# A fused attention and gated-MLP block: the first unit's queries in two pairs of heads, and the first modulation weight split along the contraction

## The chip, the cores and the metric

The kernel runs on one core of a Trainium2 chip. The core has five engines that run side by side and meet at semaphores: TensorE (matrix products, into PSUM banks), VectorE, ScalarE, GpSimd and SyncE, which here only issues DMAs. ScalarE and GpSimd issue DMAs too. Every engine takes its instructions in program order. The metric is the device time of one execution in microseconds.

## The reference

A transformer block with conditioned normalisation: attention with grouped heads (2048 queries, 32 query heads of 128 on 8 key/value heads, 2048 keys), then a gated MLP that mixes along the sequence. All inputs are bfloat16.

```
mod = (_silu(c) @ w_mod).reshape(c.shape[0], 6, 1, -1)
sa, ca, ga, sb, cb, gb = (mod[:, i] for i in range(6))
h = _layernorm(x, axis=-1) * (1 + ca) + sa
x = x + ga * _A_ref(h, A_k_cache, A_v_cache, A_wq, A_wo)
h = _layernorm(x, axis=-1) * (1 + cb) + sb
x = x + gb * _B_ref(h, B_w_in, B_w_sp, B_b_sp, B_w_out)

# _A_ref
q = (x @ wq), split into 32 heads
scores = q k^T * Dh ** -0.5
p = softmax(scores)
return (p v), heads joined, @ wo
```

What the change touches is the very start: `sa` and `1 + ca` (the first 1024 columns of `w_mod`), the normalised first rows of x, their queries for the first four heads, and the first scores.

## The kernel before

Attention runs in 128 **units**: 8 key/value heads times 16 tiles of 128 queries, each unit with its four query heads. The main loop (L1375) goes over iterations `it`; each has 8 slots. In slot i of iteration it, `qk(it, i)` makes the scores of unit `it` and ScalarE's exp of them, `pv_part` the values of the unit before, and further work is put in by hand: `later[(it, i)]` (by `at`) runs ahead of the scores of that slot, `fill[(it, i)]` behind its values. The order of each engine is the order of the program (`manual_schedule`, L634).

`qk` for unit 0 (L1024 to L1038): per slot two matmuls with the keys of one tile of 128 as weights and the queries of all four heads as 512 columns, into one of two PSUM pieces `s_ps`, and one exp of 128x1024 into `pTs[0]`. So slot i covers key tiles 2i and 2i + 1, for all four heads.

**What comes ahead of the loop.** SyncE's queue loads, in order: the first modulation weight `wmod_a` in two halves by output columns (L707; columns of `sa`, then those of `ca`), the query weight of the first group `wqs[0]` in two halves by contraction tiles (L752), the first half of the natural keys `k_nat` (L712), x tile 1 (L754), the second half of `k_nat`, x tiles 2 and 3 (L756), the other keys by a transposing DMA (L760), values and the rest of x. ScalarE's queue loads c and x tile 0 (L703, L704).

Then, on the engines:

- `warm(n)` (L784): n matmuls with zeros into a bank of `o_ps` that nobody reads. They keep TensorE at work.
- VectorE and GpSimd make the statistics of x tile 0 (`ln_stats`, L698 and L699), its 1/std (`rstd_of`, L679 and L683) and VectorE the normalised rows xn (L687).
- `mod_part` (L857): for each of the 4 output tiles of one modulation vector, 4 matmuls over the contraction, each with one column. It runs once for `sa`, once for `ca`. `mod_copy` (L867, L868) copies the one, and copies the other with 1 added.
- Four transposes of xn (L894), two scale-and-shift steps on VectorE (L816) and two on ScalarE (L908) give `hT`, the first tile of h, turned.
- Queries of all four heads (L921, 16 matmuls, in the middle of which `k_turn` turns key tiles 0 to 3, L879 and L882); VectorE copies two heads' queries and ScalarE two (L929).
- `first = dict(r1=ln1_stats(1, 1))` (L962): statistics of x tile 1.

**In iteration 0**, `first_norm` (L1198, behind the scores of slot 0) turns key tiles 4 to 7 and has the statistics of x tiles 2 and 3 and the normalised rows of tile 1; `first_turn` (ahead of slot 3) transposes tile 1 (`ln1_turn`, L834, with the scale-and-shift L816) and normalises tiles 2 and 3; `ln1_turn(2, 2)` stands ahead of slot 6. Slots 4 and 5 have the queries of tile 1 (`next_q`, L947, copied in L958), slot 7 the first of those of tiles 2 and 3 (`rest_q`). Slots 1 to 3 have one warm matmul each.

The few lines that matter most:

```
first = dict(r1=ln1_stats(1, 1))
...
def first_norm():
    k_turn((4, 5, 6, 7), (nc.vector.tensor_copy,))
    ln_stats(mv1, 2, x_sb[:, 2, :])
    first["x1"] = ln1_norm(1, 1, first["r1"])
    ln_stats(mv1, 3, x_sb[:, 3, :])
    first["r2"] = rstd_of(mv1[:, 2:4, :], 2, "ln1")
...
at(0, 3, first_turn)
at(0, 6, lambda: ln1_turn(2, 2, first["x2"]))
fill[0, 0] = [first_norm]
```

Of the kernel before, what the change touches and what calls it, by code (L numbers as in the profile page):

```python
# [12 lines left out]
ACT = mybir.ActivationFunctionType  # L13
# [562 lines left out]
def kernel(  # L576
# [93 lines left out]
    def bank(name):  # L670
        return psum.tile([P, 512], FP32, name=name)
# [30 lines left out]
    c_bf = res.tile([P, NDT], BF16, name="c_bf")  # L702
    nc.scalar.dma_start(out=c_bf[:], in_=c_dram)  # L703
    nc.scalar.dma_start(out=x_sb[:, 0, :], in_=x_dram[:, 0, :])  # L704
    for i in range(2):
        part = slice(i * D, (i + 1) * D)
        nc.sync.dma_start(out=wmod_a[:, :, part], in_=wmod_dram[:, :, part])  # L707
    k_nat = early.tile([P, SK], BF16, name="kT")

    def load_k_nat(half):  # L710
        t0, t1 = half * NKT // 4, (half + 1) * NKT // 4
        nc.sync.dma_start(  # L712
            out=k_nat[:, t0 * P : t1 * P].rearrange("p (t d) -> p t d", d=DH),
            in_=k_rows[:, t0:t1, :],
        )
# [32 lines left out]
    nc.gpsimd.memset(mhalf[:], -0.5)  # L748
    make_identity(nc, ident[:])
    wqs[0] = early.tile([P, NDT, REP * DH], BF16, name="wq_g")  # L750
    for dts in (slice(0, 2), slice(2, 4)):
        nc.sync.dma_start(out=wqs[0][:, dts, :], in_=wq_dram[:, dts, 0 : REP * DH])  # L752
    load_k_nat(0)
    nc.sync.dma_start(out=x_sb[:, 1, :], in_=x_dram[:, 1, :])  # L754
    load_k_nat(1)
    nc.sync.dma_start(out=x_sb[:, 2:CT, :], in_=x_dram[:, 2:CT, :])  # L756
# [125 lines left out]
            copy(out=kT0[:, part[0] * P : (part[-1] + 1) * P], in_=k_ps[:, 0 : n * P])  # L882


    xns0 = ln1_norm(0, 1, ln1_stats(0, 1))
    mc_ps = bank("misc")
    warm(10)
    mod_part(0, wmod_a, 0, mc_ps)
    warm(6)
    mod_part(1, wmod_a, D, mc_ps)  # L890

    x_ps = [bank("misc")[:].bitcast(BF16), bank2()[:, 0:512].bitcast(BF16)]
    for dt in range(NDT):
# [2 lines left out]
            xns0[0][:, dt * P : (dt + 1) * P],  # L896
            ident[:],
        )
    mod_copy(0, mc_ps)
    warm(2)  # L900
    hT_of(0)
    for k in range(2):
# [10 lines left out]
                    bias=modc[:, dt : dt + 1],  # L913
                )
    qTs = {0: early.tile([P, REP, 512], BF16, name="qT")}
    q_ps = [bank("misc"), bank2()]
    for dt in range(NDT):
        if dt == 2:
            k_turn((0, 1, 2, 3), (nc.vector.tensor_copy, nc.scalar.copy))
        for hh in range(REP):  # L920
            nc.tensor.matmul(  # L921
                q_ps[hh // 2][:, hh % 2 * P : (hh % 2 + 1) * P],
                lhsT=wqs[0][:, dt, hh * DH : (hh + 1) * DH],
                rhs=hTs[0][:, dt, 0:P],
                start=(dt == 0 and hh % 2 == 0),
                stop=(dt == NDT - 1 and hh % 2 == 1),
            )
    for hf, copy in enumerate((nc.vector.tensor_copy, nc.scalar.copy)):
        copy(  # L929
            out=qTs[0][:, 2 * hf : 2 * hf + 2, 0:P],  # L930
            in_=q_ps[hf][:, 0 : 2 * P].rearrange("p (h q) -> p h q", h=2),
        )
    warm(2)

    def qproj(b, heads, c0, n, banks=("misc", "misc")):

# [22 lines left out]

        return [lambda hh=hh, dt=dt: mm(hh, dt) for hh in heads for dt in range(NDT)]  # L960

    first = dict(r1=ln1_stats(1, 1))  # L962


    NU = HKV * NT
# [26 lines left out]
    def qk(u, i):  # L992
        g, j = divmod(u, NT)
        b, jj = g * NCH + j // CT, j % CT
        if i == 0:
            if homes[u] == "wsp":
                pTs[u] = wspp.tile([P, NT, 512], BF16, name="wsp")
            else:
                pTs[u] = late.tile([P, NKT, 512], BF16, name=homes[u], bufs=1)
            if by_rows(u):  # L1000
                rsums[u] = stat.tile([P, NSLOT], FP32, name="rs")
        s_ps = bank2()
        if by_rows(u):
            hh, half = divmod(i, 2)
            for c in range(2):
                k0 = (2 * half + c) * 512
                nc.tensor.matmul(  # L1007
                    s_ps[:, c * 512 : (c + 1) * 512],
                    lhsT=qTs[b][:, hh, jj * P : (jj + 1) * P],
                    rhs=groups[g]["kT"][:, k0 : k0 + 512],  # L1010
                    start=True,
                    stop=True,
                )
            nc.scalar.activation(  # L1014
                out=rows_of(u, hh)[:, half * HK : (half + 1) * HK],
                in_=s_ps[:],
                func=ACT.Exp,
                scale=inv_sqrt_dh,
                accum_out=rsums[u][:, i : i + 1],
            )  # L1020
            if half == 1:
                at(*divmod(u * NSLOT + i + 2, NSLOT), lambda: turn_rows(u, hh))
            return
        for h in range(2):  # L1024
            kt = 2 * i + h
            nc.tensor.matmul(  # L1026
                s_ps[:, h * 512 : (h + 1) * 512].rearrange("p (r q) -> p r q", r=REP),
                lhsT=groups[g]["kT"][:, kt * P : (kt + 1) * P],
                rhs=qTs[b][:, :, jj * P : (jj + 1) * P],
                start=True,  # L1030
                stop=True,
            )
        nc.scalar.activation(  # L1033
            out=pTs[u][:, 2 * i : 2 * i + 2, :],
            in_=s_ps[:].rearrange("p (k q) -> p k q", k=2),
            func=ACT.Exp,
            scale=inv_sqrt_dh,
        )  # L1038
# [157 lines left out]

    fill = {}
    def first_norm():  # L1198
        k_turn((4, 5, 6, 7), (nc.vector.tensor_copy,))
        ln_stats(mv1, 2, x_sb[:, 2, :])  # L1200
        first["x1"] = ln1_norm(1, 1, first["r1"])
        ln_stats(mv1, 3, x_sb[:, 3, :])
        first["r2"] = rstd_of(mv1[:, 2:4, :], 2, "ln1")
# [386 lines left out]
```

## Time and profile before

| | us |
|---|---|
| median of 3 runs | 1311.61 (1310.94 to 1311.62) |
| the profiled execution | 1311.72 |
| its span, first to last instruction | 1309.7 |
| first modulation weight, first half, used by TensorE from | 5.40 |
| its second half, from | 7.43 |
| first scale-and-shift (L816) | 8.36 |
| first score matmul of unit 0 (L1026) | 10.63 |
| first exp (L1033) | 11.26 |
| first score matmul of unit 1 | 18.36 |

All times within the profile count from the start of the span. A row of a timeline gives an instruction's start, its length, engine, line, operation, what it writes and reads, and in brackets how long its engine had been idle before it and what ended that. Consecutive like instructions are put together ("x6"): then the length is from the first one's start to the last one's end. On TensorE the ends are modelled: the next matmul starts before the shown end of the one before, so the step from start to start is what a matmul costs in a stream. A chain of waits is followed back from the last instruction of the execution: each piece was released by the one above it. A row of waits gives the total, how many there were, and the longest.

### The profile page before, as it was taken

To read this page: it belongs to the slowest core of one execution; us is meant where nothing else is said; L and a number is where in the kernel's file an instruction comes from. 1 tells how busy PE (TensorE), PEld (TensorE's weight loads), DVE (VectorE), ACT (ScalarE), POOL (GpSimd) and SP (SyncE) were. 2 spreads that over 40 slices of the span, in tenths; PEclk is the share of its full clock that TensorE was granted. 3 is DMA by queue.
4 is the path that set the end of the run, shared out by engine and by line. 5 is a ranking of instruction groups with operands and counts; after the bars stand their busy time and mean duration, and the time that the engine had idled before them with its cause. 6 is when DMAs were issued, how large, how long until landed. Compare 5 with 4: busy or idle time off the path is not lost.

```text
span 1309.7 us, 24370 instructions
## 1 busy us (share of the span) xinstructions
PE 1301.9 (99%) x9527; PEld 736.3 (56%) x9527; DVE 684.2 (52%) x1693; ACT 1112.4 (85%) x1533; POOL 58.7 (4%) x116
## 2 busy tenths in 40 slices
PE   9999999999999999999999999999999999999998
PEld 5665555555555555555555555555555555644445
DVE  6544544444445454444454544444555588784443
ACT  7899999999999999999999999999999999550000
POOL 1200000000000000000000000000000011120000
PEclk9999999999999999999999999999999999999999
DMA  7668778877887677867986678678776688464300
GB/s 181 153 94 154 129 127 159 154 126 133 153 168 143 126 139 155 145 130 137 169 160 127 125 156 156 128 137 153 163 144 124 119 141 147 105 134 96 85 21 31
DMA packets 607723, 174.45 MB, mean 133 GB/s; under 512 B 597264, under 2 KB 603664, under 8 KB 607600
## 3 DMA queue, kind: packets, MB, share of 16 engines
q1 hardware_dynamic: 600576, 153.67, 65.0%
q0 software_dynamic: 4432, 16.91, 4.2%
q10 hardware_dynamic: 2592, 2.23, 0.5%
q8 instruction: 77, 1.26, 0.4%
q14 instruction: 46, 0.38, 0.1%
HBM read 21.89 MB, written 2.10 MB: 18 GB/s over the span
## 4 chain that ended last, share of the span: by engine, by line
PE 97%; DMA 2%; DVE 1%; POOL 0%; issue 0%; ACT 0%; SPq 0%; DVEq 0%
PE o_ps L1082 18%; PE s_ps L1026 18%; PE s_ps L1007 16%; PE o_ps L1061 16%; PE misc L1114 8%; PE misc L947 8%; PE misc L1457 7%; PE s_ps L1292 2%; PE s_ps L1331 2%; PE o_ps L1490 1%; DMA wsp<-in_w_mod_dram 1%; PE s_ps L1490 0%; DMA wmod_a<-in_w_mod_dram 0%; DMA hT<-xn 0%; DVE hT L816 0%; DVE bnst L698 0%
## 5 line engine op out<-in xcount | busy, mean ns | idle before, releaser
L1033 ACT ACTIVATE pT<-s_ps 128x1024 bf16<-128x1024 f32 x552 | 560.4, 1024 | 32.1 <-PE s_ps L1026 10.1
L1082 PEld LDWEIGHTS <-pT 128*128 128x128 bf16 x4416 | 295.3, 98 | 128.9
L1082 PE MATMUL o_ps<-v,pT 128*128 128x129 bf16 x4416 | 339.7, 220 | 0.0
L1026 PE MATMUL s_ps<-qT,kT 128*128 128x512 bf16 x1104 | 328.1, 379 | 0.3 <-ACT pT L1033 0.2
L1007 PE MATMUL s_ps<-kT,qT 128*128 128x512 bf16 x944 | 280.7, 379 | 0.1
L1014 ACT ACTIVATE win_sb<-s_ps 128x1024 bf16<-128x1024 f32 x238 | 243.4, 1024 | 3.5
L1114 PE MATMUL misc<-wo_g,oT 128*128 128x512 bf16 x512 | 194.0, 379 | 0.0
L947 PE MATMUL misc<-hT,wq_g 128*128 128x512 bf16 (+2 forms) x520 | 187.0, 371 | 0.1
L1026 PEld LDWEIGHTS <-kT 128*128 128x128 bf16 x1104 | 107.2, 98 | 115.0 <-issue 2.3
L1014 ACT ACTIVATE pn<-s_ps 128x1024 bf16<-128x1024 f32 x156 | 159.4, 1023 | 2.0 <-ACT wmod_a L1014 0.3
L1061 PEld LDWEIGHTS <-v 128*128 128x128 bf16 x944 | 92.3, 98 | 111.5
L958 DVE CAST qT<-misc 128x512 bf16<-128x512 f32 x125 | 85.6, 685 | 123.5 <-PE misc L947 123.5
L1070 DVE CAST oT<-o_ps 128x512 bf16<-128x512 f32 x59 | 40.8, 691 | 195.0 <-PE o_ps L1061 195.0
L1061 PE MATMUL o_ps<-wsp,v 128*128 128x512 bf16 x480 | 142.1, 379 | 0.0
L1061 PE MATMUL o_ps<-pT,v 128*128 128x512 bf16 x464 | 138.0, 379 | 0.0
L1007 PEld LDWEIGHTS <-qT 128*128 128x128 bf16 x944 | 92.2, 98 | 61.7 <-issue 0.2
L1047 DVE TENSOR_TENSOR tot<-rs 128x1 f32<-128x1 f32 x236 | 36.1, 153 | 127.3 <-ACT win_sb L1014 84.9
L1457 PE MATMUL misc<-wsp,z 128*128 128x512 bf16 (+2 forms) x560 | 100.5, 336 | 0.0
L1052 DVE TENSOR_SCALAR win_sb<-win_sb,rall 128x2048 bf16<-128x2048 bf16 x119 | 89.6, 753 | 4.4 <-DVE rall L1050 0.3
L1014 ACT ACTIVATE wmod_a<-s_ps 128x1024 bf16<-128x1024 f32 x78 | 79.8, 1023 | 0.0
L1457 PEld LDWEIGHTS <-z 128*128 128x128 bf16 x560 | 50.5, 98 | 48.4 <-issue 0.2
L1127 DVE TENSOR_TENSOR xacc<-misc,xacc 128x512 f32<-128x512 f32 x112 | 76.0, 679 | 0.0
(111 smaller groups left out, 817.4 us busy)
## 6 DMA issues: line engine op xcount, KB each, us to landing
v<-in_A_v_cache_dram POOLq DMA_DIRECT2D x7, 512.0 KB, 6.6
wq_g<-in_A_wq_dram POOLq DMA_DIRECT2D x7, 512.0 KB, 4.9
wo_g<-in_A_wo_dram POOLq DMA_DIRECT2D x7, 512.0 KB, 4.3
wsp<-in_w_mod_dram POOLq DMA_DIRECT2D x1, 2048.0 KB, 11.8
out_dram<-yout ACTq DMA_DIRECT2D x16, 128.0 KB, 1.7
win_sb<-in_B_w_in_dram POOLq DMA_DIRECT2D x1, 1792.0 KB, 8.1
x_sb<-in_A_x_dram SPq DMA_DIRECT2D x3, 512.0 KB, 8.1
oT<-onorm SPq DMA_TRANSPOSE x69, 2.8
```

The source lines that it names most:

```text
L947: nc.tensor.matmul(ps[0][:, o0 : o0 + n], lhsT=wqs[g][:, dt, hh * DH : (hh + 1) * DH], rhs=hTs[ch][:, dt, c0 : c0 + n], start=(dt == 0), s ...
L958: nc.vector.tensor_copy(out=dst, in_=src)
L1007: nc.tensor.matmul(s_ps[:, c * 512 : (c + 1) * 512], lhsT=qTs[b][:, hh, jj * P : (jj + 1) * P], rhs=groups[g]["kT"][:, k0 : k0 + 512], sta ...
L1014: nc.scalar.activation(out=rows_of(u, hh)[:, half * HK : (half + 1) * HK], in_=s_ps[:], func=ACT.Exp, scale=inv_sqrt_dh, accum_out=rsums[u ...
L1026: nc.tensor.matmul(s_ps[:, h * 512 : (h + 1) * 512].rearrange("p (r q) -> p r q", r=REP), lhsT=groups[g]["kT"][:, kt * P : (kt + 1) * P], ...
L1033: nc.scalar.activation(out=pTs[u][:, 2 * i : 2 * i + 2, :], in_=s_ps[:].rearrange("p (k q) -> p k q", k=2), func=ACT.Exp, scale=inv_sqrt_dh,)
L1052: nc.vector.tensor_scalar(out=rows, in0=rows, scalar1=rinv, scalar2=None, op0=ALU.mult)
L1061: nc.tensor.matmul(o_pss[u][:], lhsT=groups[g]["v1"][:, kt, 0:DH], rhs=pTs[u][:, kt, :], start=(kt == 0), stop=(kt == NKT - 1),)
L1082: nc.tensor.matmul(o_ps[:, hh % 2, 0 : DH + 1], lhsT=pTs[u][:, kt, hh * P : (hh + 1) * P], rhs=groups[g]["v1"][:, kt, 0 : DH + 1], start=( ...
L1114: nc.tensor.matmul(X_ps[:], lhsT=oTs[u][:, hh, :], rhs=groups[g]["wo"][:, hh, :], start=(hh == 0), stop=(hh == REP - 1),)
L1127: nc.vector.tensor_tensor(out=xaccs[j][:], in0=X_ps[:], in1=xaccs[j][:], op=ALU.add)
L1457: nc.tensor.matmul(g_pss[f][:, :n], lhsT=z2[:, st, f * P : (f + 1) * P], rhs=wsp[t][:, st, c0 : c0 + n], start=(st == 0), stop=(st == NT - ...
```

## The change

The first modulation weight is loaded as three contraction tiles (all 1024 columns) and then the last one, instead of two halves of the columns. `mod_first(kt)` makes the 8 one-column matmuls of one contraction tile; with the first tile goes a matmul of a matrix of 1/128 with ones, which puts the added 1 into the columns of `ca`. Three tiles run ahead of the transposes of x tile 0, the last behind them, and one copy replaces the two.

The first group's query weight is loaded by pairs of heads, in rows of 256 columns, with the first half of the natural keys between the two. `first_q(hf)` makes and copies the queries of one pair, always on VectorE. The first pair is made ahead of the loop, the second in `first_norm`, behind the scores of slot 0. Unit 0's `qk` goes by pairs: slot i has four key tiles and the pair i % 2, four matmuls of 256 columns. Key tiles 0 and 1 are copied by ScalarE and 2 and 3 by VectorE (the other way round before). The statistics of x tile 1 move from ahead of the loop into `first_norm`, behind the copy of key tiles 4 to 7.

```diff
--- before.py
+++ after.py
@@ -702,9 +702,8 @@
     c_bf = res.tile([P, NDT], BF16, name="c_bf")
     nc.scalar.dma_start(out=c_bf[:], in_=c_dram)
     nc.scalar.dma_start(out=x_sb[:, 0, :], in_=x_dram[:, 0, :])
-    for i in range(2):
-        part = slice(i * D, (i + 1) * D)
-        nc.sync.dma_start(out=wmod_a[:, :, part], in_=wmod_dram[:, :, part])
+    for kts in (slice(0, NDT - 1), slice(NDT - 1, NDT)):
+        nc.sync.dma_start(out=wmod_a[:, kts, :], in_=wmod_dram[:, kts, 0 : 2 * D])
     k_nat = early.tile([P, SK], BF16, name="kT")
 
     def load_k_nat(half):
@@ -748,9 +747,10 @@
     nc.gpsimd.memset(mhalf[:], -0.5)
     make_identity(nc, ident[:])
     wqs[0] = early.tile([P, NDT, REP * DH], BF16, name="wq_g")
-    for dts in (slice(0, 2), slice(2, 4)):
-        nc.sync.dma_start(out=wqs[0][:, dts, :], in_=wq_dram[:, dts, 0 : REP * DH])
+    pairs = [slice(2 * hf * DH, 2 * (hf + 1) * DH) for hf in range(2)]
+    nc.sync.dma_start(out=wqs[0][:, :, pairs[0]], in_=wq_dram[:, :, pairs[0]])
     load_k_nat(0)
+    nc.sync.dma_start(out=wqs[0][:, :, pairs[1]], in_=wq_dram[:, :, pairs[1]])
     nc.sync.dma_start(out=x_sb[:, 1, :], in_=x_dram[:, 1, :])
     load_k_nat(1)
     nc.sync.dma_start(out=x_sb[:, 2:CT, :], in_=x_dram[:, 2:CT, :])
@@ -882,12 +882,30 @@
             copy(out=kT0[:, part[0] * P : (part[-1] + 1) * P], in_=k_ps[:, 0 : n * P])
 
 
+    def mod_first(kt, mc_ps):
+        for col in range(2 * NDT):
+            nc.tensor.matmul(
+                mc_ps[:, col : col + 1],
+                lhsT=wmod_a[:, kt, col * P : (col + 1) * P],
+                rhs=sc_bf[:, kt : kt + 1],
+                start=(kt == 0 and col == 0),
+                stop=(kt == NDT - 1 and col == 2 * NDT - 1),
+            )
+        if kt == 0:
+            nc.tensor.matmul(
+                mc_ps[:, NDT : 2 * NDT],
+                lhsT=mean_bf[:],
+                rhs=ones_bf[:, 0:NDT],
+                start=False,
+                stop=False,
+            )
+
     xns0 = ln1_norm(0, 1, ln1_stats(0, 1))
     mc_ps = bank("misc")
-    warm(10)
-    mod_part(0, wmod_a, 0, mc_ps)
-    warm(6)
-    mod_part(1, wmod_a, D, mc_ps)
+    warm(12)
+    for kt in range(NDT - 1):
+        mod_first(kt, mc_ps)
+    warm(1)
 
     x_ps = [bank("misc")[:].bitcast(BF16), bank2()[:, 0:512].bitcast(BF16)]
     for dt in range(NDT):
@@ -896,7 +914,8 @@
             xns0[0][:, dt * P : (dt + 1) * P],
             ident[:],
         )
-    mod_copy(0, mc_ps)
+    mod_first(NDT - 1, mc_ps)
+    nc.vector.tensor_copy(out=modc[:, 0 : 2 * NDT], in_=mc_ps[:, 0 : 2 * NDT])
     warm(2)
     hT_of(0)
     for k in range(2):
@@ -913,24 +932,26 @@
                     bias=modc[:, dt : dt + 1],
                 )
     qTs = {0: early.tile([P, REP, 512], BF16, name="qT")}
-    q_ps = [bank("misc"), bank2()]
-    for dt in range(NDT):
-        if dt == 2:
-            k_turn((0, 1, 2, 3), (nc.vector.tensor_copy, nc.scalar.copy))
-        for hh in range(REP):
-            nc.tensor.matmul(
-                q_ps[hh // 2][:, hh % 2 * P : (hh % 2 + 1) * P],
-                lhsT=wqs[0][:, dt, hh * DH : (hh + 1) * DH],
-                rhs=hTs[0][:, dt, 0:P],
-                start=(dt == 0 and hh % 2 == 0),
-                stop=(dt == NDT - 1 and hh % 2 == 1),
-            )
-    for hf, copy in enumerate((nc.vector.tensor_copy, nc.scalar.copy)):
-        copy(
+
+    def first_q(hf):
+        q_ps = bank("misc")
+        for dt in range(NDT):
+            for k in range(2):
+                hh = 2 * hf + k
+                nc.tensor.matmul(
+                    q_ps[:, k * P : (k + 1) * P],
+                    lhsT=wqs[0][:, dt, hh * DH : (hh + 1) * DH],
+                    rhs=hTs[0][:, dt, 0:P],
+                    start=(dt == 0 and k == 0),
+                    stop=(dt == NDT - 1 and k == 1),
+                )
+        nc.vector.tensor_copy(
             out=qTs[0][:, 2 * hf : 2 * hf + 2, 0:P],
-            in_=q_ps[hf][:, 0 : 2 * P].rearrange("p (h q) -> p h q", h=2),
+            in_=q_ps[:, 0 : 2 * P].rearrange("p (h q) -> p h q", h=2),
         )
-    warm(2)
+
+    first_q(0)
+    k_turn((0, 1, 2, 3), (nc.scalar.copy, nc.vector.tensor_copy))
 
     def qproj(b, heads, c0, n, banks=("misc", "misc")):
 
@@ -959,7 +980,7 @@
 
         return [lambda hh=hh, dt=dt: mm(hh, dt) for hh in heads for dt in range(NDT)]
 
-    first = dict(r1=ln1_stats(1, 1))
+    first = {}
 
 
     NU = HKV * NT
@@ -1021,6 +1042,23 @@
             if half == 1:
                 at(*divmod(u * NSLOT + i + 2, NSLOT), lambda: turn_rows(u, hh))
             return
+        if u == 0:
+            k0, qs = i // 2 * 4, slice(i % 2 * 256, (i % 2 + 1) * 256)
+            for kt in range(4):
+                nc.tensor.matmul(
+                    s_ps[:, kt * 256 : (kt + 1) * 256].rearrange("p (r q) -> p r q", r=2),
+                    lhsT=groups[g]["kT"][:, (k0 + kt) * P : (k0 + kt + 1) * P],
+                    rhs=qTs[b][:, i % 2 * 2 : i % 2 * 2 + 2, 0:P],
+                    start=(kt % 2 == 0),
+                    stop=(kt % 2 == 1),
+                )
+            nc.scalar.activation(
+                out=pTs[u][:, k0 : k0 + 4, qs],
+                in_=s_ps[:].rearrange("p (k q) -> p k q", k=4),
+                func=ACT.Exp,
+                scale=inv_sqrt_dh,
+            )
+            return
         for h in range(2):
             kt = 2 * i + h
             nc.tensor.matmul(
@@ -1196,7 +1234,9 @@
 
     fill = {}
     def first_norm():
+        first_q(1)
         k_turn((4, 5, 6, 7), (nc.vector.tensor_copy,))
+        first["r1"] = ln1_stats(1, 1)
         ln_stats(mv1, 2, x_sb[:, 2, :])
         first["x1"] = ln1_norm(1, 1, first["r1"])
         ln_stats(mv1, 3, x_sb[:, 3, :])
```

## The prediction

> **What bounds the kernel now.** I read the busy times first, then TensorE's waits, then the chain that ended last in order of time, then the first 20 us engine by engine.
>
> ```profile
> PE 1301.9 (99%) x9527; PEld 736.3 (56%) x9527; DVE 684.2 (52%) x1693; ACT 1112.4 (85%) x1533; POOL 58.7 (4%) x116
> ```
>
> ```profile
> PE o_ps L788 <- DVE onorm L769: 1.2, 1, 1.2
> PE misc L857 <- DMA wsp<-in_w_mod_dram: 0.7, 1, 0.7
> PE s_ps L1026 <- ACT pT L1033: 0.2, 1, 0.2
> PE misc L857 <- DMA wmod_a<-in_w_mod_dram: 0.2, 1, 0.2
> ```
>
> TensorE is the bound, and these are all its waits (total, times, longest). From 18.52 us on, the chain is TensorE's own stream: each step of the second unit takes 1.10 us (18.52, 19.62, 20.73), and its score, value and query matmuls (0.43 + 0.45 + 0.22) add up to that. So a change of the first stage counts through one number only: when the second unit's first score matmul starts, at 18.36 us. The chain up to there (start, length, what):
>
> ```profile
> 1.48 5.91 DMA wmod_a<-in_w_mod_dram
> ...
> 7.43 0.57 PE misc L857 x16
> ...
> 16.23 0.69 DVE qT L958
> 16.93 1.28 DVE hT L816 x4
> 18.21 0.04 issue
> 18.25 0.27 PE misc L947
> ```
>
> It begins with the modulation weight and ends on VectorE: four scale-and-shift steps of tiles 2 and 3, with the last query matmul right behind the last of them. ScalarE has its exps early:
>
> ```profile
> 11.26 5.61 ACT L1033 ACTIVATE pT<-s_ps 128x1024 bf16<-128x1024 f32 x6 [0.68 <-PE s_ps L1026]
> ```
>
> Six follow without a gap; the next had to wait until 17.11. So VectorE's order is the thing to follow. Its timeline (start, length):
>
> ```profile
> 10.10 0.42 DVE L929 CAST qT<-misc 128x256 bf16<-128x256 f32 x1 [0.16 <-PE misc L921]
> 10.44 0.68 DVE L698 BATCH_NORM_STATS2 bnst<-x_sb 128x6 f32<-128x512 bf16 x1
> 11.15 0.18 DVE L699 BATCH_NORM_AGGREGATE mv<-bnst 128x2 f32<-128x6 f32 x1
> 11.48 0.42 DVE L882 COPY kT<-o_ps 128x512 bf16<-128x512 bf16 x1
> 11.82 0.68 DVE L698 BATCH_NORM_STATS2 bnst<-x_sb 128x6 f32<-128x512 bf16 x1
> 12.54 0.18 DVE L699 BATCH_NORM_AGGREGATE mv<-bnst 128x2 f32<-128x6 f32 x1
> 12.64 0.38 DVE L687 TENSOR_SCALAR xn<-x_sb,mv,rstd_ln 128x512 bf16<-128x512 bf16 x1
> ...
> 14.99 0.73 DVE L687 TENSOR_SCALAR xn<-x_sb,mv,rstd_ln 128x512 bf16<-128x512 bf16 x2 [0.17 <-POOL rstd_ln L683]
> 16.23 0.69 DVE L958 CAST qT<-misc 128x512 bf16<-128x512 f32 x1 [0.51 <-PE misc L947]
> ```
>
> Tile 1's statistics sit at 10.44, in the time in which TensorE makes the first scores, and its row normalisation xn at 12.64 is done at 13.02. TensorE's transposes of it start at 13.08, ahead of the fourth score step.
>
> **Part 1, the modulation.** The same 1 MB in the same two issues, cut 768 + 256 KB. The halves reached TensorE at 5.40 and 7.43, so 256 KB take about 1.0 us: the first piece is there at 6.4, the second at 7.4 as before. Twelve warm matmuls instead of ten (0.42 us each at first, 0.22 later) end at 5.7, under that wait. Then 25 narrow matmuls at 26 ns (16 ran from 5.40 to 5.82) make 0.65 us, to 7.06; one warm, to 7.27; four transposes of xn (0.055 each, 7.85 to 8.07 before), to 7.49; then the last eight, 0.20, where sixteen took 0.41 before. The separate addition (0.08, the step from 8.02 to 8.10) goes; its matmul is one of the 25. From the start of the last group to the first scale-and-shift (call it A; 7.43 to 8.36 before, 0.93) it is now 0.93 - 0.20 - 0.08 = 0.65. So A = 7.49 + 0.65 = 8.14.
>
> xn must be there at 7.27. It ends at 7.08 (6.67 + 0.41), 2.34 us after x tile 0 landed at 4.74. That tile comes by ScalarE's queue beside the modulation weight, whose rows are now 2 KB instead of 1 KB. Bounds for A: 8.01 if the tile is as early as before and the weight earlier (xn at 7.08, a handoff of 0.06, transposes 0.22, then 0.65); 8.51 if the tile is 0.5 later. I take 8.2, near the computed end: 0.16 earlier than 8.36.
>
> **Part 2, the first pair.** All from A. The last scale-and-shift of tile 0 ends at +0.80 (ScalarE's two from 8.35, 0.81). Two matmuls behind it and their latency: VectorE's cast starts at +1.16 and frees VectorE at +1.50 (0.34, as 10.10 to 10.44). ScalarE copies key tiles 0 and 1, VectorE 2 and 3, +1.50 to +1.79 (0.29). The last two of four 256-wide score matmuls (0.11 each) start at +1.89, and with 0.27 of latency the first exp starts at +2.32. Before it was 11.26, +2.90: a gain of 0.58.
>
> **Part 3, the second pair.** It is now behind the first scores on TensorE: eight matmuls from +2.11, 0.44, ending at +2.72. VectorE, in order, waits for it from +1.79 to +2.75 with nothing to do; tile 1's statistics, which filled this time, stand behind it. Then: cast 2.75 to 3.09; copy of key tiles 4 to 7, 0.34, to 3.43; statistics of tile 1, 0.82 (11.82 to 12.64), to 4.25, with their result at 4.33; GpSimd's rstd 0.98 later (11.33 to 12.31 before), 5.31; VectorE does tile 2's statistics to 5.07 and waits; xn of tile 1 from 5.35 to 5.73. Before, it started at 12.64, that is +4.28. It is **1.07 us later** after A.
>
> TensorE stands at the transposes for about 1.2 us; behind it wait the fourth score step, ScalarE's exp of it, and all later query matmuls. From there the order and forms are those of before: statistics of tile 3, four scale-and-shifts, xn of tiles 2 and 3, cast, four scale-and-shifts, last query matmul. Nothing in that run is slack: its two small waits (0.17 for GpSimd, 0.51 for TensorE) are links of the same sequence. So the second unit starts at A + 11.07 instead of 8.36 + 10.00.
>
> The exps of unit 0 cover the same 128x1024 each; score matmuls double in number and halve in width (8 x 4 x 0.11 against 8 x 2 x 0.22). No cost. The warm matmuls taken out (16 to 13 ahead of the transposes, and two behind the queries) stood in waits and cost nothing either way.
>
> **Part 4, the query weight.** 256 KB twice as before, in rows of 512 B instead of 1 KB. The two landed at about 8.1 and 8.8 (6.0 us after issues at 2.13 and 2.8). Bounds: nothing, or twice the 0.7 us each if a row costs the same whatever its length. Pair 0 lands at 8.1 to 8.8 and is needed at A + 0.40 = 8.6; the key rows, issued one place sooner, before 9.2 and needed at 9.2; pair 1 by 10.5 and needed at 10.3. So 0 to +0.4 us. I take 0: at the rate of the nearest rows, its own before, all are in time. Later loads on this queue keep their place.
>
> **Sum.** -0.16 + 1.07 = +0.91 us. The profiled execution took 1311.72 (span 1309.7 and 2.0 around it), so 1312.63; against the median of 1311.61 it is **1312.5**. A measurement of this kernel tells about 0.2% (2.6 us) from no change, so this counts as no change, on the slower side.
>
> **Rivals.** *ScalarE sets the pace of unit 0*, and the earlier first exp is kept: -0.58 - 0.16, 1310.9. For it: six exps without a gap. Against: the seventh waited, and the chain into 18.25 is VectorE's. 0.10.
>
> *The lateness is swallowed at 48.9 us*, where TensorE waits 0.7 us for the other modulation weights: 1311.8. For it: the wait is real. Against: that load is issued at 37.04 by GpSimd behind a chain of VectorE and transposes that starts with the same late steps, so it moves too. 0.10.
>
> *Tile 0 of x is late.* If the 2 KB rows beside it hold it up by 0.5 us, xn is at 7.58 and A at 8.51: +1.22, 1312.8; with the full 0.4 of part 4, 1313.2. For it: both queues load at once until 4.74. Against: bytes per us may be shared evenly. 0.14. The Trainium skill, "DMA: Bandwidth & Descriptors", section "Queues, rings and completion order", says that an engine takes turns between queues by packet, which speaks for this rival; no row of before has 2 KB rows here.
>
> *TensorE's clock falls back*, the slower side beyond the bound. Its warm matmuls took 0.42 us at first and 0.22 from about 5 us, after 3.8 us of work. New idle stretches are 0.7 us at 5.7 and 1.2 us at the transposes. If the second brings the slow clock for another 3.8 us, half the work in it, 1.9 us, is added: +2.8, 1314.4. Against: 0.24 us waits at 12.3 left the pace of 0.22 alone, though no idle of 1.2 us is shown. 0.06. The Trainium skill, "TensorE: Matmul & The Clock Gate", section "What's actually happening", asks for about 3.4 us of idleness before the clock drops; by it this rival adds nothing. No row of before can show that.
>
> **Chances.** Forecast 0.58, rivals as given, 0.02 for what I haven't seen. The forecast's own range is 1312.3 to 1313.0. For 8 in 10 it is widened to 1310.9 for the two lower rivals and for the spread of the runs (0.7), and to 1314.0 for late inputs with the same spread. Slower by over 0.2% (above 1314.2): the clock case and a little of the unseen, 0.07; faster by over 0.2%: 0.03, since no wait of this size is there to remove; within: 0.90.
>
> **What would show it.** First exp near 10.5; VectorE idle for about 1 us before the second pair's cast; xn of tile 1 near 13.5 to 13.9; TensorE idle for about 1 us ahead of L834's first transposes; the second unit's first scores near 19.3. If these come before 18.4, the order of VectorE is not the bound and I am wrong; if xn of tile 0 ends after 7.4, part 1 is.

## The result, and the profile after

The changed kernel took 1315.79 us (median of 7 runs, 1314.23 to 1320.4), the kernel before 1310.94 (median of 7 runs beside it, 1310.26 to 1311.65): ratio 1.004, 95% interval 1.003 to 1.005. It is slower, as forecast, but by 4.9 us and not by 0.9, and outside the range.

The profiled execution took 1315.47, with a span of 1313.4. Two profiles of the kernel before are used below: the one shown above (span 1309.7) and a second (called b_again, span 1308.7), taken beside the experiments. Busy times of the changed kernel, from its page:

```profile
PE 1302.2 (99%) x9539; PEld 739.1 (56%) x9539; DVE 685.4 (52%) x1693; ACT 1112.6 (85%) x1532; POOL 59.1 (4%) x116
```

No engine has more work to speak of (TensorE +0.3 us), so the time went into waits and into pace. TensorE's waits of more than 0.3 us (total, times, longest):

```profile
PE o_ps L788 <- DVE onorm L769: 1.2, 1, 1.2
PE misc L912 <- DVE xn L687: 1.2, 1, 1.2
PE misc L834 <- DVE xn L687: 1.1, 1, 1.1
PE misc L1497 <- DVE gb L1524: 0.7, 1, 0.7
```

The first is in the kernel before too. The second, ahead of the transposes of x tile 0, and the fourth, in the gated MLP at the far end, were not forecast. The third, ahead of the transposes of tile 1, was. The chain that ended last now begins with another load (start, length, what):

```profile
1.19 4.62 DMA x_sb<-in_A_x_dram
5.83 0.71 DVE bnst L698
...
8.23 0.23 PE misc L912
...
9.54 1.01 PE misc L941 x8
...
19.90 1.28 DVE hT L816 x4
21.18 0.04 issue
21.23 0.27 PE misc L968
21.50 0.43 PE s_ps L1064 x2
```

Tile 0 of x stands where the modulation weight stood, and eight query matmuls of 128 columns (L941) take 1.01 us, twice the 0.44 that I took for the eight of part 3. It ends as before, on VectorE's scale-and-shifts, but the second unit's scores stand at 21.33 (they were at 18.36, and at 18.09 in b_again). VectorE's timeline shows the way there (start, length; in brackets the idle time ahead of it and what ended that):

```profile
3.60 0.17 DVE L773 CAST c_f<-c_bf 128x4 f32<-128x4 bf16 x1 [2.35 <-DMA c_bf<-in_c_dram]
5.83 0.69 DVE L698 BATCH_NORM_STATS2 bnst<-x_sb 128x6 f32<-128x512 bf16 x1 [1.00 <-DMA x_sb<-in_A_x_dram]
7.76 0.41 DVE L687 TENSOR_SCALAR xn<-x_sb,mv,rstd_ln 128x512 bf16<-128x512 bf16 x1 [1.02 <-POOL rstd_ln L683]
9.05 0.59 DVE L816 TENSOR_SCALAR hT<-misc,modc 128x128 bf16<-128x128 bf16 x2
...
12.99 0.42 DVE L948 CAST qT<-misc 128x256 bf16<-128x256 f32 x1 [1.69 <-PE misc L941]
13.33 0.42 DVE L882 COPY kT<-o_ps 128x512 bf16<-128x512 bf16 x1
13.66 0.68 DVE L698 BATCH_NORM_STATS2 bnst<-x_sb 128x6 f32<-128x512 bf16 x1
...
15.58 0.41 DVE L687 TENSOR_SCALAR xn<-x_sb,mv,rstd_ln 128x512 bf16<-128x512 bf16 x1 [0.22 <-POOL rstd_ln L683]
```

Tile 0 is used at 5.83 instead of 4.74, so A, the first scale-and-shift, is at 9.05 instead of the forecast 8.2. Then VectorE idles 1.69 us for the second pair, and tile 1's statistics stand behind that, as forecast. The same points in b_again, on VectorE and TensorE:

```profile
4.93 0.70 DVE L698 BATCH_NORM_STATS2 bnst<-x_sb 128x6 f32<-128x512 bf16 x1 [0.99 <-DMA x_sb<-in_A_x_dram]
...
8.14 0.59 DVE L816 TENSOR_SCALAR hT<-misc,modc 128x128 bf16<-128x128 bf16 x2
...
1304.02 0.43 DVE L1503 TENSOR_TENSOR yout<-tmp,x_sb 128x512 bf16<-128x512 bf16 x1
```

```profile
18.09 0.59 PE L1026 MATMUL s_ps<-qT,kT 128*128 128x512 bf16 x2
```

The second unit's first scores in after:

```profile
21.33 0.59 PE L1064 MATMUL s_ps<-qT,kT 128*128 128x512 bf16 x2
```

The spans of after and of b_again differ by 4.70 us, and five points of the two traces divide this without a rest:

| stretch | b_again | after | difference |
|---|---|---|---|
| start to A | 8.14 | 9.05 | +0.91 |
| A to the second unit's first scores | 9.95 | 12.28 | +2.33 |
| from there to the attention's last row-sum step | | | +0.00 |
| from there to the MLP's first bias step (gb, L1524) | 86.01 | 86.77 | +0.76 |
| from there to the last output tile (yout), rest of the same | | | 0.00 |
| last yout to the end of the span | 4.66 | 5.36 | +0.70 |

The 0.00 of the third row holds against b_again alone. In before's first profile this stretch is 0.92 us longer, with the wait of 0.7 us for the other modulation weights in it, and the spans differ by 3.65 us and not by 4.70. b_again, at 1310.67, is the nearer one to the median.

The forecast knew the first two rows alone. The experiments first divide the second row, then find the cause of the first, and then of the two at the end.

### The profile page after: what moved, and what is told of

Read it like the earlier page. It is cut to its first block, busy times and chain, and to the rows that moved or that the text cites. A ratio compares the mean times of both kernels' runs of the same rounds, so it can differ in the third digit from the quotient of the medians.

```text
span 1313.4 us, 24391 instructions
## 1 busy us (share of the span) xinstructions
PE 1302.2 (99%) x9539; PEld 739.1 (56%) x9539; DVE 685.4 (52%) x1693; ACT 1112.6 (85%) x1532; POOL 59.1 (4%) x116
## 4 chain that ended last, share of the span: by engine, by line
PE 96%; DVE 2%; DMA 1%; POOL 1%; issue 0%; ACTq 0%; ACT 0%; DVEq 0%; POOLq 0%
PE o_ps L1120 19%; PE s_ps L1064 18%; PE s_ps L1028 16%; PE o_ps L1099 16%; PE misc L1152 8%; PE misc L968 8%; PE misc L1497 7%; PE s_ps L1332 1%; PE o_ps L1530 1%; DVE stz L1354 1%; DMA xnT<-xn 0%; PE s_ps L1530 0%; DVE z L687 0%; DMA x_sb<-in_A_x_dram 0%; POOL rstd_lnz L683 0%; PE s_ps L1048 0%
## 5 line engine op out<-in xcount | busy, mean ns | idle before, releaser
L1071 ACT ACTIVATE pT<-s_ps 128x1024 bf16<-128x1024 f32 x544 | 553.6, 1025 | 29.5 <-PE s_ps L1064 7.7
L1064 PE MATMUL s_ps<-qT,kT 128*128 128x512 bf16 x1088 | 323.5, 379 | 0.0
L1035 ACT ACTIVATE pn<-s_ps 128x1024 bf16<-128x1024 f32 x156 | 159.6, 1024 | 2.0 <-ACT pn L1035 0.3
L1035 ACT ACTIVATE wmod_a<-s_ps 128x1024 bf16<-128x1024 f32 x78 | 79.9, 1024 | 0.3 <-ACT wmod_a L1035 0.3
```

Source lines behind the costliest of these rows:

```text
L1035: nc.scalar.activation(out=rows_of(u, hh)[:, half * HK : (half + 1) * HK], in_=s_ps[:], func=ACT.Exp, scale=inv_sqrt_dh, accum_out=rsums[u ...
L1064: nc.tensor.matmul(s_ps[:, h * 512 : (h + 1) * 512].rearrange("p (r q) -> p r q", r=REP), lhsT=groups[g]["kT"][:, kt * P : (kt + 1) * P], ...
L1071: nc.scalar.activation(out=pTs[u][:, 2 * i : 2 * i + 2, :], in_=s_ps[:].rearrange("p (k q) -> p k q", k=2), func=ACT.Exp, scale=inv_sqrt_dh,)
```

## Experiments

Times are medians; "before" beside them was 1311.08 (24 runs), 1311.02 (27) and 1310.96 (29) in three groups of runs. Diffs are against the changed kernel unless said otherwise.

**e1_stats_early: tile 1's statistics put back where they stood**, ahead of the second pair's cast.

```diff
-    first = {}
+    first = dict(r1=ln1_stats(1, 1))
...
-        first["r1"] = ln1_stats(1, 1)
```

> The changed kernel with the statistics of x tile 1 back ahead of the loop, between VectorE's copy of key tiles 2 and 3 and the copy of the second pair's queries. Theory of VectorE's order: they fit in the idle 1 us there, xn of tile 1 ends about 1.1 us sooner after the first scale-and-shift, and the second unit's first score matmul comes about 1.0 us sooner than in the changed kernel (near 20.1 instead of 21.1 us); the time falls by about 1 us, to 1314.8. Rival, the half clock alone sets this stage: xn comes sooner, the second unit does not by more than 0.3 us. In both the half clock after 9 us stays.

1314.48 (8 runs, 1313.44 to 1317.44), ratio 1.003 [1.0019, 1.0041]. A at 9.01, second unit at A + 11.16: 1.12 earlier than in after. The first stage still ran at half pace for a while (granted clock, the share of its full speed that TensorE has, 0.50 from 9.81 to 13.22 us).

**e2_rows_1k: the modulation weight in rows of 1 KB again**, with the split along the contraction kept.

```diff
-        nc.sync.dma_start(out=wmod_a[:, kts, :], in_=wmod_dram[:, kts, 0 : 2 * D])
+        for cols in (slice(0, D), slice(D, 2 * D)):
+            nc.sync.dma_start(out=wmod_a[:, kts, cols], in_=wmod_dram[:, kts, cols])
```

> The changed kernel with each of the two pieces of the first modulation weight loaded as two column halves, so rows of 1 KB instead of 2 KB and the same split along the contraction. Theory that the 2 KB rows hold up the loads on ScalarE's queue: x tile 0 is used at about 4.8 us (5.83 in the changed kernel), c at about 2.5 (3.6), the first scale-and-shift comes near 8.2 (9.05), the idle 1.3 us ahead of the transposes goes, with it the half clock, and the time is the forecast one, 1312.5. Rival, the earlier issue of the other SyncE loads holds x tile 0 up: it is still used near 5.8 and the time stays at 1315.

1314.97 (6 runs, 1312.65 to 1317.14), ratio 1.0031 [1.0019, 1.0043]. In its profile TensorE had full clock in the first stage, and this is the first stage that I had forecast. VectorE, then TensorE:

```profile
4.92 0.69 DVE L698 BATCH_NORM_STATS2 bnst<-x_sb 128x6 f32<-128x512 bf16 x1 [0.24 <-DMA x_sb<-in_A_x_dram]
8.13 0.59 DVE L817 TENSOR_SCALAR hT<-misc,modc 128x128 bf16<-128x128 bf16 x2
10.93 0.42 DVE L949 CAST qT<-misc 128x256 bf16<-128x256 f32 x1 [1.01 <-PE misc L942]
13.52 0.41 DVE L687 TENSOR_SCALAR xn<-x_sb,mv,rstd_ln 128x512 bf16<-128x512 bf16 x1 [0.23 <-POOL rstd_ln L683]
```

```profile
13.99 0.28 PE L835 MATMUL misc<-ident,xn 128*128 128x128 bf16 x2 [1.12 <-DVE xn L687]
19.29 0.59 PE L1065 MATMUL s_ps<-qT,kT 128*128 128x512 bf16 x2
```

Tile 0 is in time again at 4.92 (b_again: 4.93), so the way in which the modulation weight is loaded made it late. Two things change here at once: the rows (1 KB for 2) and the loads (384 and 128 KB for 768 and 256). Beside loads of 512 KB in rows of 1 KB the tile is in time too (b_again), which speaks for the rows; no run has 768 KB in rows of 1 KB. The load of c stays late (used at 3.46, for 3.60 in after and 2.50 in b_again), so its delay has another cause, which was not looked for. The rest, A + 11.16 for the second unit, is the order of VectorE by itself.

The median is 2.5 us above the 1312.5 that was expected. The profiled run took 1313.89, with 1.2 us lost in the MLP and 0.8 at the end (below); the slower runs have a lower mean clock (0.996 to 0.998).

**e3_warm_fill: seven warm matmuls instead of one** ahead of the transposes of tile 0, to fill TensorE's idle time there.

```diff
-    warm(1)
+    warm(7)
```

> The changed kernel with seven warm matmuls instead of one ahead of the transposes of x tile 0, 1.3 us of work in the wait for xn. Theory that this idle stretch brings the half clock: no matmul at the 0.107 us pace after 9 us, first exp about 0.9 us sooner (near 11.4 instead of 12.3), time lower by about 0.9 us and the spread of the runs (6.2 us in the changed kernel) under 2 us. Rival, the clock falls for another reason: the same half clock near 9.3 to 12.7 and the same spread. x tile 0 stays late in both.

1314.51 (10 runs, 1313.64 to 1315.5), ratio 1.0027 [1.0017, 1.0036]. One stretch of after and of e3, from the view of windows (stretch; length, busy time of PE, PEld, DVE, ACT, POOL with counts, granted clock, DMA share, GB/s):

```profile
9.20:12.70 3.50, 2.97 (x24) 2.44 (x24) 1.16 (x4) 1.43 (x4) 0.00 (x0) 0.51 1.32 243
```

```profile
9.20:12.70 3.50, 2.58 (x32) 2.12 (x32) 1.92 (x7) 2.12 (x4) 0.00 (x0) 1.00 1.31 211
```

In after the granted clock is 0.51 and 24 matmuls take 2.97 us; in e3 it is 1.00 and 32 take 2.58. Its second unit is at A + 11.14. So 12.28 - 11.14 = 1.14 us of the second row was pace, and the rest order. The two add up: early statistics save 1.12 us with the clock low (after to e1) and 1.13 with it full (e6 to e7, below).

**e4_pairs_only and e5_mod_only: one part each.** e4 is the kernel before with the pairs of heads and the order that comes with them, and the modulation weight in its old halves with its added 1 on its own. e5 is the kernel before with part 1 alone. The core of e4's diff, which takes part 1 out again:

```diff
-    for kts in (slice(0, NDT - 1), slice(NDT - 1, NDT)):
-        nc.sync.dma_start(out=wmod_a[:, kts, :], in_=wmod_dram[:, kts, 0 : 2 * D])
+    for i in range(2):
+        part = slice(i * D, (i + 1) * D)
+        nc.sync.dma_start(out=wmod_a[:, :, part], in_=wmod_dram[:, :, part])
...
-    mod_first(NDT - 1, mc_ps)
-    nc.vector.tensor_copy(out=modc[:, 0 : 2 * NDT], in_=mc_ps[:, 0 : 2 * NDT])
+    mod_copy(0, mc_ps)
```

> The kernel before with the pairs of heads alone (query weight by pairs, unit 0's scores by pairs, statistics of tile 1 behind the second pair), the modulation as before. Theory of the forecast: first scale-and-shift as before near 8.4, first exp 0.6 us sooner (near 10.7), xn of tile 1 1.07 us later, second unit's first scores near 19.4 (18.36 before), time 1312.0. Rival, the pairs are harmless and all the loss is the modulation's: second unit by 18.6, time within 0.3 us of before.

1313.0 (11 runs, 1311.8 to 1313.85), ratio 1.0015 [1.0006, 1.0024]. Tile 0 used at 4.78, A at 8.67, second unit at A + 11.13. The time is 1.0 us above the 1312.0 expected: A is 0.3 later than thought, and the MLP lost 0.8 us (below).

> The kernel before with the modulation part alone (weight split along the contraction, added 1 by a matmul, transposes ahead of the last eight matmuls). Theory that x tile 0 is held up by the 2 KB rows: it is used at 5.8 us, first scale-and-shift near 9.05 (8.36 before), second unit's first scores 0.7 us later than before (19.05), up to 19.9 where the half clock comes; time 1311.5 to 1312.5. Rival, the part itself is a gain and only the pairs lose: second unit by 18.2.

1313.9 (11 runs, 1312.12 to 1315.49), ratio 1.0023 [1.0014, 1.0032]. Tile 0 used at 5.74, A at 8.96, second unit at A + 9.96. So each part belongs to one term: part 1 to the late tile, the pairs to the order. Part 1 costs more by the median (2.9 us, against 1.5 at most expected) than by its profile (span 1310.1, its fastest run). Its mean clock over a run was 0.997 to 0.999, against 0.999 to 1.0 in e4, so a lower clock comes with part 1; where in the run it is low, the means don't show, and the profiled run had full clock in the first stage.

**b_again: the kernel before, unchanged**, for a second profile.

> The kernel before, unchanged, for a second profile of it. In the runs so far three things outside the first 20 us differ from the one profile of before: TensorE no longer waits 0.7 us at 48.9 us for the second modulation weights; the MLP's first bias step comes 86.5 to 87.3 us after the last row-sum step (86.0 before); the span ends 5.3 us after the last output tile is computed in four of five runs (4.5 before). If these belong to the change, this profile has again the wait, 86.0 and 4.5. If they are chance of the transfers, at least one of them is different here.

One time, 1310.67. A at 8.14, second unit at A + 9.95. So A itself differs by 0.2 us between two executions of one program.

**e6_x0_first: tile 0 of x loaded by SyncE's queue, ahead of the modulation weight.**

```diff
-        nc.scalar.dma_start(out=x_sb[:, 0, :], in_=x_dram[:, 0, :])
+        nc.sync.dma_start(out=x_sb[:, 0, :], in_=x_dram[:, 0, :])
```

> The changed kernel with x tile 0 as the first load of SyncE's queue instead of the second of ScalarE's. Theory: x tile 0 is used by 3.6 us, its xn is there long before the modulation weight, and the first scale-and-shift is set by the weight's last piece: near 7.7 (9.05 in the changed kernel). The second unit's first scores come 11.1 us behind that (the late statistics stay): near 18.8 without the half clock, time 1311.5 to 1312.5. Rival, something else holds the first scale-and-shift: it stays above 8.3.

1312.3 (11 runs, 1311.5 to 1313.02), ratio 1.0007 [0.9998, 1.0016]. Tile 0 used at 3.97, A at 7.98, clock full, second unit at A + 11.15.

**e7_both_mended: e6 and e1 together**, and two warm matmuls more ahead of the first query matmuls (`warm(2)` to `warm(4)`).

> The changed kernel with x tile 0 first on SyncE's queue, the statistics of tile 1 back ahead of the loop, and four warm matmuls instead of two ahead of the first scale-and-shift. If these two are the whole loss: first scale-and-shift near 7.7, xn of tile 1 about 4.4 behind it, second unit's first scores near 17.8 (18.36 before), time 1310.6, under the kernel before. Rival, the half clock or the score matmuls of unit 0 in pairs cost by themselves: second unit at 18.4 or later and no gain.

1310.98 (11 runs, 1310.04 to 1312.94), ratio 0.9997 [0.9988, 1.0006]: no difference from before. VectorE, then TensorE:

```profile
7.73 0.59 DVE L816 TENSOR_SCALAR hT<-misc,modc 128x128 bf16<-128x128 bf16 x2
...
9.58 0.69 DVE L698 BATCH_NORM_STATS2 bnst<-x_sb 128x6 f32<-128x512 bf16 x1
...
10.53 0.42 DVE L948 CAST qT<-misc 128x256 bf16<-128x256 f32 x1
...
12.02 0.38 DVE L687 TENSOR_SCALAR xn<-x_sb,mv,rstd_ln 128x512 bf16<-128x512 bf16 x1
```

```profile
17.75 0.59 PE L1064 MATMUL s_ps<-qT,kT 128*128 128x512 bf16 x2
```

The statistics (9.58) fill the time in which VectorE would wait for the second pair (10.53), and the second unit is at A + 10.02. Its first exp is at 10.08, A + 2.35, half a microsecond sooner than before's A + 2.90; nothing of this reaches the second unit.

**e8_thin_14: the kernel before with 14 more matmuls**, of one column of zeros, behind `warm(6)`. The pairs bring 12 to 14 matmuls more too. It asks whether the loss in the MLP comes from the length of TensorE's program alone.

```diff
     warm(6)
+    thin(14)
     mod_part(1, wmod_a, D, mc_ps)
```

> The kernel before with 14 one-column matmuls of zeros (0.35 us in all) in TensorE's wait for the second half of the modulation weight: 28 instructions more on TensorE, as many as the pairs of heads bring, and nothing else. Theory that the loss in the MLP is a matter of where TensorE's program is fetched: the 16 KB instruction transfer comes near 52.3 us after the last row-sum step, between the transposing loads and the load of the output weights, as in all seven runs with pairs (55 to 58 in the three without); the first bias step comes at 86.5 or later instead of 86.0, and the time rises by 0.5 to 1 us at an unchanged second unit (18.1 to 18.4). Rival, the pairs act there in another way: 86.0 and the time of before.

1311.73 (11 runs, 1310.78 to 1313.09), ratio 1.0005 [0.9996, 1.0014]; the second unit at 18.22, so the first stage is untouched. In its profile the MLP lost about what it loses in after (0.9 us, for 0.8). TensorE's wait, and VectorE's step that is late ahead of it, of e8:

```profile
PE misc L1465 <- DVE gb L1492: 0.8, 1, 0.8
```

```profile
1165.79 0.98 DVE L1166 TENSOR_SCALAR hT<-xnT,modc 128x128 bf16<-128x128 bf16 x4 [4.98 <-DMA xnT<-xn]
```

The same step in after, and in b_again:

```profile
1168.60 0.98 DVE L1196 TENSOR_SCALAR hT<-xnT,modc 128x128 bf16<-128x128 bf16 x4 [4.68 <-DMA xnT<-xn]
```

```profile
1163.94 0.98 DVE L1158 TENSOR_SCALAR hT<-xnT,modc 128x128 bf16<-128x128 bf16 x4 [3.26 <-DMA xnT<-xn]
```

VectorE waits for a transposing load, 3.26 us in b_again and 4.7 to 5.0 in the other two. SyncE issues that load behind transposing loads of another weight. What is new among those, in 1 us of each trace (queue, packets, MB, share of the DMA engines), in after and in e8:

```profile
q1 hardware_dynamic: 219, 0.05, 22.3%
q8 instruction: 1, 0.02, 6.2%
```

```profile
q1 hardware_dynamic: 318, 0.07, 33.1%
q8 instruction: 1, 0.02, 6.1%
```

One fetch of 16 KB of instructions, on queue q8, falls among the transposing loads, 52.2 to 52.4 us after the last row-sum step, in every kernel that has 12 to 14 matmuls more than before; b_again, before, e5 and e9 have it at 55.2 to 58.5, behind them. The first bias step stands at 86.0 where the fetch comes late, and at 86.5 to 87.5 in the kernels with pairs (in e3, with 18 matmuls more, the fetch is at 51.0 and the step at 86.5; e11, below, is the exception); in e8 it stands at 86.90. The output weights, whose load starts there too, took 8.3 us to land in after, 8.8 in e8 and 7.1 in b_again.

SyncE's own rows show where the fetch falls. Its four issues of the other weight that begin 50.2 us after the last row-sum step take 6.94 us in after, 7.71 in e8 and 6.42 in b_again:

```profile
1155.14 6.94 SPq L1228 DMA_TRANSPOSE wsp<-in_B_w_sp_dram  x4
```

```profile
1151.90 6.42 SPq L1190 DMA_TRANSPOSE wsp<-in_B_w_sp_dram  x4
```

The second of the four, at 51.5 on the same count, takes 2.1 to 2.3 us instead of 1.25 in all seven kernels with the fetch at 52.2 to 52.3. With the fetch at 51.0 (e3) it is the one at 50.2 instead, and with 48.7 (e11) the one at 49.0, both over 2.0. Only e4, with the fetch at 52.4, has no long one there. So the long issue goes with the fetch; how it grows into VectorE's longer wait was not followed.

**e9_mod_x0_first: e5 with tile 0 of x first on SyncE's queue**; part 1 without pairs.

> The kernel before with the modulation part alone and x tile 0 first on SyncE's queue; no pairs. First scale-and-shift near 7.75, second unit's first scores 10.0 behind it, near 17.75; first bias step 86.0 behind the last row-sum step, since TensorE has no instructions more. Time 1310.3 if the end of the span is as in the kernel before (4.5 us behind the last output tile); ScalarE has 2117 instructions here, the number at which the end took 5.3 in four runs, and if that number is the cause it is 5.3 here and the time 1311.1. Rival, the late first tile is not what the modulation part lost: second unit above 18.4.

1311.6 (11 runs, 1311.0 to 1312.45), ratio 1.0004 [0.9995, 1.0013]. A at 7.54, second unit at A + 9.96, 0.86 us sooner than in before's first profile; the end of the span is 5.43 behind the last output tile, instead of 4.52 in e5, and takes it back. Against b_again the second unit is 0.59 us sooner, and 1.03 us go besides in the stretch with the wait for the other modulation weights, which this kernel has too (0.8 us).

**e10_act_one_more: the changed kernel with one more copy on ScalarE**, ahead of the exp of the modulation's input, to test whether this tail of 5.4 us goes by the length of ScalarE's program.

```diff
+    nc.scalar.copy(out=en[:], in_=c_f[:])
```

> The changed kernel with one more small copy on ScalarE, ahead of the exp of c. Theory that the late end (5.3 us behind the last output tile) hangs on where ScalarE's program ends: it goes back to 4.5, and the time falls by 0.8, to 1315.0. Rival, the end is late because of the change's transfers or by chance: 5.3 stays. The first 20 us as in the changed kernel, half clock and its spread included.

1315.38 (7 runs, 1312.61 to 1319.31), ratio 1.0036 [1.0023, 1.0048]. The tail is 4.51 instead of 5.36. The last output tile of after, then of e10 (spans 1313.4 in both):

```profile
1308.03 0.42 DVE L1543 TENSOR_TENSOR yout<-tmp,x_sb 128x512 bf16<-128x512 bf16 x1
```

```profile
1308.89 0.42 DVE L1544 TENSOR_TENSOR yout<-tmp,x_sb 128x512 bf16<-128x512 bf16 x1
```

The tile is written 0.86 us later (the MLP lost 0.7 us more, to 87.48), and the span ends at the same time. The median cannot show it: the runs spread over 6.7 us, with mean clocks of 0.997 to 1.000.

In the half microsecond from 2.1 to 2.6 us behind the start of the last output tile, the view of DMA in after shows one more fetch of instructions:

```profile
q14 instruction: 1, 0.01, 7.2%
```

The four other traces with a tail of 5.3 to 5.4 us (e1, e2, e3, e9) have it there too, and none of the nine with 4.5 to 4.7 us has it. So the longer tail comes with a fetch more; that it waits for it is not shown.

**e11_mended_thin: e7 with 13 matmuls more** (`warm(1)` to `thin(14)`), to move the fetch of instructions ahead of the transposing loads.

> The version with x tile 0 first and the statistics back ahead, with 14 one-column matmuls in the place of the one warm ahead of the transposes: 26 instructions more on TensorE. Theory of the fetch: the instruction transfer moves from 52.2 to near 49.3 us after the last row-sum step, ahead of the load of the output weights; if it does no harm there, the first bias step is back at 86.0 and the time at 1310.3 (1310.98 without). Rival: 86.7 stays, time 1311.

1311.19 (11 runs, 1310.04 to 1311.94), ratio 1.0001 [0.9992, 1.001]. In its profile the fetch comes at 48.7, the first bias step is at 86.05, the second unit at 17.57 and the span is 1308.1, the shortest of all. The median shows no gain: its profiled run was the fastest of the eleven, and what the other ten lost was not traced. VectorE's wait for the transposing load is 4.1 us here, 3.9 in e5 and 3.6 in e9, and the step stands at 86.0 to 86.05 in all three, so the MLP loses nothing by a wait that long; with 4.6 to 5.4 it loses.

## Why the prediction was wrong, point by point

| term | forecast | measured (after against b_again) |
|---|---|---|
| part 1: A | 0.16 earlier | 0.91 later |
| parts 2 and 3: order of VectorE | +1.07 | +1.18 to 1.21 (e2, e3, e4, e6) |
| TensorE's clock | a rival, 0.06 | +1.14 |
| part 4 | 0 | 0 seen |
| the MLP | not seen | +0.76 |
| the end | not seen | +0.70 |

**The step that failed is in part 1: "xn must be there at 7.27. It ends at 7.08".** The 2.34 us from the tile to the end of xn held (5.83 to 8.17). The landing of the tile did not. I had the rows of 2 KB beside it as a rival with 0.5 us, and the tile came 1.1 us later than in the first profile of before. The sign that the prediction named for this, xn of tile 0 ending after 7.4, came: 8.17. The loads of the changed kernel, and of b_again (KB each, us to landing):

```profile
wmod_a<-in_w_mod_dram SPq DMA_DIRECT2D x1, 768.0 KB, 4.7
...
wmod_a<-in_w_mod_dram SPq DMA_DIRECT2D x1, 256.0 KB, 5.3
...
x_sb<-in_A_x_dram ACTq DMA_DIRECT2D x1, 128.0 KB, 4.6
...
c_bf<-in_c_dram ACTq DMA_DIRECT2D x1, 1.0 KB, 2.9
```

```profile
wmod_a<-in_w_mod_dram SPq DMA_DIRECT2D x2, 512.0 KB, 5.2
...
x_sb<-in_A_x_dram ACTq DMA_DIRECT2D x1, 128.0 KB, 3.8
...
c_bf<-in_c_dram ACTq DMA_DIRECT2D x1, 1.0 KB, 1.8
```

Both loads of ScalarE's queue lost 0.8 to 1.1 us; the one of c is not what A waited for, since VectorE was done with c at 4.83, a microsecond before the tile came. TensorE used the first piece of the weight at 6.05 and had no wait for the second. My 7.08 for xn was too early: the tile became the last thing to wait for. The Trainium skill, "DMA: Bandwidth & Descriptors", section "Queues, rings and completion order", has the engines take turns by packet; the 3.8 and 4.6 agree with it in sign. e5 shows that the delay comes with part 1 alone, and e2 that rows of 1 KB, in smaller loads, take it away.

With the tile no earlier than before, part 1 gains nothing: e2 has A at 8.13, b_again, without part 1, at 8.14, and in e2 TensorE still waits 0.2 us for xn. With the tile first as well, A is at 7.54 (e9), 0.60 sooner; how much of that is the split is not shown, since the old halves were not run with the tile first. The tail of part 1 is shorter as worked out (last group of the modulation to A: 0.59 in after, for 0.65), but the transposes now wait for xn instead. The 8.36 from which I counted was itself one execution of several: 8.14 to 8.67 in the profiles with the old halves.

**Parts 2 and 3 were right to a tenth.** e2, with full clock in its first stage, has the first exp at A + 2.36 (forecast 2.32), VectorE idle for 1.01 (0.96), xn of tile 1 at A + 5.39 (5.35), TensorE waiting 1.12 ahead of the transposes (1.2) and the second unit at A + 11.16 (11.07). With the statistics back in their place e7 has 10.02. So VectorE's order was the bound, and the rival in which ScalarE sets the pace falls: e7 has its first exp half a microsecond sooner after A, and the second unit not at all.

**The clock** was a rival of 0.06, with the wrong place and about the right size. I looked at the 1.2 us at tile 1's transposes; it fell after the 1.17 us at tile 0's, which the late tile opened. The 1.1 us at tile 1's left the clock at 1.00 in after, e2, e3, e4 and e6. The length of the slow stretch was 3.4 us (forecast 3.8), the loss 1.14 (1.9). It differs between runs: the two runs of after with a mean clock of 1.000 took 1314.23 and 1314.25, that with 0.996 took 1320.4, and two with 0.997 took 1315.47 and 1318.29. The prediction also put the warm matmuls that the change takes out at nothing, since they "stood in waits"; e3, with six of them more, has the 1.14 us back. The Trainium skill, "TensorE: Matmul & The Clock Gate", section "What's actually happening", asks for about 3.4 us of idleness; here the clock fell behind a wait of 1.17 us, and in e1 of 0.9, though not in the profile of e5 behind one of 1.7. The measurement decides, and I had let the Trainium skill take the weight off this rival. That filling the wait removes it is shown by e3 in its profile and by its spread (1.9 us for 6.2).

Which waits count is open. In after, e1 and e10 the granted clock rises at 5.82, 6.40 and 5.95 us and falls 3.41 us later in each, for 3.41 us, with the wait in between. In e5 it rises at 4.26, and the wait, from 6.43 to 8.14, lies across the point 3.41 us behind that. This would fit a clock that is set anew every 3.41 us, and would make runs differ; no run moves the wait, so it is not shown. Not explained either is e2, whose slower runs have a low mean clock although its tile was in time.

**The swallowing at 48.9 us** did not happen in after: there is no wait there to swallow anything. The wait is no fixed part of the kernel: it is 0.6 to 0.8 us in before's first profile, e5 and e9, and b_again, e8 and the kernels with pairs don't show it.

**The MLP and the end** were outside what I looked at, and this is a second step that failed: "a change of the first stage counts through one number only", the start of the second unit. "From there the order and forms are those of before" was taken to hold to the end of the span. The order did hold: the stretch from the second unit to the last row-sum step is the same as in b_again to 0.01 us. Yet 1.46 us came 1150 us later. e8 shows that 14 matmuls that do nothing cost the MLP 0.9 us in a profile; its median, +0.77, has an interval that includes no change, so by the time alone this is not settled. For the tail, after, e1, e2, e3 and e9 have 5.3 to 5.4 us behind the last output tile and all have 2117 ScalarE instructions in the trace (with the waits, branches and DMA issues that the page does not count as busy); those with 2116, 2118 or 2119 have 4.5 to 4.7. It came as expected in e9 and e10. What ends later in those 0.8 us was not isolated; the fetch shown under e10 is the lead.

The terms add up for the undisturbed runs also: 0.91 + 1.19 + 0.76 + 0.70 = 3.56, and 1310.94 + 3.56 = 1314.5, beside the 1314.24 of the two runs at full clock.

## What to carry to other kernels

Before an instruction is moved behind a wait, look at what stands behind it in its engine's order: the statistics of tile 1 were free ahead of the second pair and cost 1.1 us behind it, while the earlier exps bought nothing, because they were not what came last. Loading a weight in larger rows made the small tile beside it 0.9 us late here, so give the tile that is needed first its own place at the head of the queue: with that and the statistics back (e7), the change costs nothing, and gains nothing. When a sum is of the order of 1 us, count also the waits in which TensorE's clock may fall, and the length of each engine's program.

## What was not expected of the hardware

- Beside a weight loaded in rows of 2 KB (768 and 256 KB), a tile of 128 KB on another queue took 4.6 us to land, and beside rows of 1 KB 3.8 (b_again, two loads of 512 KB) and 3.7 (e2, four smaller loads).
- TensorE's granted clock was 0.51 for 3.4 us behind waits of 0.9 to 1.3 us (e1, after, e10), and stayed full behind one of 1.7 (e5).
- 14 more matmuls of one column moved a fetch of 16 KB of instructions among transposing loads 1150 us later: one issue beside it took 2.2 us instead of 1.25, and VectorE's wait for a later one was 5.0 us instead of 3.3.
- One ScalarE instruction more or less changed the tail behind the last output tile between 4.5 and 5.4 us (e10; e9 against e5).
